# Row variance of the later layer norms from a centred square on ScalarE, in place of a raw square and two small VectorE operations

## The chip, the cores and the metric

The kernel runs on one core of a Trainium2 chip. A core has five engines that run their own instruction queues: TensorE (PE, matrix products; its weight loads are listed apart as PEld), VectorE (DVE), ScalarE (ACT), GpSimd (POOL) and SyncE (SP, which issues most of the DMAs). They wait for one another through semaphores. The metric is the device time of one execution in microseconds. The kernel before took 319.8 us, the median of three runs (319.6 to 320.18).

## The reference

The input x has 2048 rows of 512 numbers (bf16). Four layers follow each other, each of the form x = x + layer(norm(x)), in the order A, B, A, B with the same weights for both A and both B layers. The norm is what the change touches:

```python
def _layernorm(x, axis=-1, eps=1e-5):
    m = jnp.mean(x, axis=axis, keepdims=True)
    v = jnp.var(x, axis=axis, keepdims=True)
    return (x - m) / jnp.sqrt(v + eps)
```

Layer A is linear attention with 32 heads of 16 channels: q, k and v from one projection, q and k multiplied by a small matrix per head and passed through two softmaxes (of the values and of their negatives), then products of the features with v, a division by the denominators, and an output product. Layer B is sliding-window attention: each position looks at itself and seven earlier positions, two apart, with a softmax over the eight, and an output product. The result is x after the fourth layer.

## The kernel before

The rows are cut into four blocks of 512 rows, and a block into four tiles of 128 rows (one row per partition). All of x stays on chip. Every layer is a set of stages per block: a norm, projections, the attention's own steps, and an output product that adds the residual. The stages of a layer are a1 (k, v and the sums over rows), a2 (q), a3 and a4 (denominators and output) for A, and b1 (q, k, v), b2 (scores and softmax), b3 (values) for B. The output product of all layers is `s_out` (line 531). For every layer but the last it also gathers what the next layer's norm needs, so there are twelve such norms: three layer boundaries of four blocks. The first layer's norms get their statistics in another way (`s_ln_first`) and are not touched.

In `s_out`, for each of a block's four tiles t: `mm` multiplies on TensorE into a bank of PSUM; `res` adds the residual and writes x back, on VectorE (line 571) or, where TensorE has added the residual by an identity product (line 556), on ScalarE (line 568). Both also leave the row's sum in one column of `sums`. `sq` (line 574) squares the tile on ScalarE and leaves the row's sum of squares in a column of `ss`; it waits for `res`. The squared tile itself, `sqd`, is thrown away. After the four tiles, `var` (line 584) forms ss - sums * sums / 512 for all four columns on VectorE with two operations on 128x4 numbers. `s_norm` (line 443) goes on: `ln` takes the logarithm of the variance plus eps and an exponential with factor -0.5 on ScalarE (lines 450 and 453), which gives rstd; `nmr` forms -mean * rstd on VectorE (line 457); `ap` writes the normalised tile xn, on VectorE (line 466) or ScalarE (line 468); then xn is transposed to xnT, by a DMA from the SP queue (line 473) or by TensorE (line 482) with copies out of PSUM (lines 202 and 204). The projections of the next layer read xnT.

ScalarE and VectorE share the copies out of PSUM (`copy`, lines 202 and 204); a string of digits, `_CHOICE`, fixes for each copy which of the two does it. PSUM has eight banks, and another string, `_SLOTS`, gives each product its bank; a product waits until the bank's earlier content has been read. ScalarE also does all exponentials (lines 638, 745, 1073) and VectorE the large products of layer B (lines 1059 and 1121).

The order of each engine's work is written out by hand: `_ORDER` (line 60) is a list of 1492 tokens, each the next step of one named thread, and an engine takes its instructions in the order of that list. A stage's steps on one engine form a thread; `var` and `nmr` of a norm are two tokens of the same thread.

Of the kernel before, what the change touches and what calls it, by code (L numbers as in the profile page):

```python
# [60 lines left out]
8 2 i 2e 3s e3 ce 2p 23 i a 5l i i 9 i i i 5o i i i i 4e e7 1m i 0 3u 3r 0 f i e c j b 2 k 3 4 j o 5q 1m l 3 m
p 1n 0 i 1 n 1t e4 o 1o q 1m 1p r 0 1m 1u s 1m z 5k z z 5 1m 1r 7 6 z 20 20 7 1q 1s 1t 21 21 t 20 20 1v 22 10
z 22 1t 7 1t 20 1w 22 t 11 24 24 13 u 12 16 12 1t t 15 1t v 12 12 22 x 18 14 1x d w w 1y 2c y 18 18 26 18 2d
1f 2d 2c 1z 2d 24 2d 27 17 19 18 1a 1b 21 1c 1d 22 21 22 39 1e 20 20 22 39 25 2c 3b 3a 3a 1f 3a 2d 3a 2f 2c 1f
1f 39 ch 22 2f 2d 2g 1g 29 1f 2d 1j 2f 2d 7 1h 29 1i 1k 3a 29 2n 29 2i 2n 3c 2o 2o 2o 2k 2o 2k 2q 1l cd 2h 2n
2a 2k 2f 2n 2k 3a 2o 2j 24 2q 2r 2q 2o 2o 2o 29 2y 28 2y 2y 3c 2l 2z 2v 2z 2s 2z 2z 2k 2y 2z 39 36 31 2z 36 2z
3a 3b 36 36 2v 31 2v 37 2v 31 2t 36 2z 36 2b 2b 2b 2b 2m 2m ci 36 36 2m 3a 2w 2m 2v 33 34 32 31 3c 35 2q 3c 36
3b 2x g 2x 2u 2x 30 37 2x 36 38 38 38 38 3i 3c 3h 3c 39 3b 3a 3j 3k 3k 3k 3c 3d 3c 3e 3l 3b 3m 3d 3e 5h 3n 3m
3c 3e 3e 3l 5i 3m 3q 3m 3m 4f 3m 3d 3l 5j 3e 3e 3m 5i 3m 3m 3v 3d 3e 3e bd 5h 5m 5n 5i 5i 5i 3m 3d 3e 7c 5h 7d
5p 5i 5i 5i 5r 3f 3g 3g 5i 3f 3g 5i 3w 3f 3z 3x 3f 3g 5s 3y 7e 40 41 3g 7d 5u 5v 7f 5t 3g 3p 41 42 41 41 44 3g  # L70
43 3g 43 5w 5x 5x 7f 45 46 43 43 47 43 7f 5y 3f 90 47 48 49 3g 4c 91 5x 41 4b 41 41 41 4a 92 5x 4d 60 91 4l 5z
61 5z 93 5z 4q 62 5z 4g 7d 4g 4g 4m 4q 63 ck 5z 7d 4r 93 4i 4l 63 66 64 67 7g 4s 7j 65 7h 7i 4h 4j 7k bo 4n 4q
4q 4u 4w 91 7l 4t 7l 7l 7m 7l 7o 68 7n 7n 4l 7p 3h 7n 7q 4w 93 4v 7n 4v 3o 91 4f 6a 7r 4o 6b 7n 6k 6f 69 4g 4k
4l 7r 6l 7s h 4w 6g 6k 6m 4p 6a 6c 6p 7t 7u 6a 6k 6f 6n 7v 4w 6k 6h 94 6r 6d 4x 4x b2 6r 4x 97 6o 98 4x 95 6f
69 7x 96 99 99 9a 4y 6i 99 7w 9b 6q 9c 6q 9d 9b 9b 99 9e 9b 6r 6a 6e 6f 6j 83 84 d4 6q 7y 9f 7y 9b 6r 6s 6s 6s
6s 9f 9h 9i 4y 9g 4w 8d 80 9j 7z 6t 6t 3t 88 6s 83 89 6t 88 88 88 8a 8b 8f 8c 7y 6r 7x 4x 9l 6u 9k 6u 4y 6u 4w
6q 6u 83 85 83 86 87 81 9r 9w 7y 9w 9s 9x 4v 82 4v 9w 6v 9y 9z 4z a1 6v 4z 6v 6w 4z 8e 6v 4z 6y 9m 6x 6z 70 9n
70 70 71 72 73 70 9m 74 72 72 8e 9m 50 50 50 75 50 9o 72 51 9r 52 76 53 8f 54 55 72 9p 9w 76 8f 79 55 77 7a 9r
9t 55 58 78 7b 9u 55 9r 56 9m 8f 59 8g 57 5a 57 8e 8g a3 8g 8g 57 bz b0 8e 9q 57 9v a0 5b 57 8h a3 5b bz 8h a3
8g 5d c0 5e 5c 5f c0 c0 b0 c0 bz 8h b1 5g b3 b1 8f b0 b1 b3 a2 b1 a4 c0 b1 a4 b1 a3 a4 a2 a4 b4 b5 a5 bz a5 8i  # L80
8i c0 8i a2 b3 a4 a2 c0 bx b6 c0 b3 a5 by bx by by b0 b7 bx by by by a3 8i bx 8j 8j b1 8j 8l a6 8k 8j 8m b1 8n
ap by aq aq ap a6 aq aq 8o 8o 8p by 8r 8o 8o 8q 8s 8q as 8t 8q as ap 8q au as ap a6 8u 8q a7 aq at 8u 8w aq bz
a7 8v a7 aq aq 8x 8y 8z bx a9 a6 a7 a8 b8 aa as ax b8 ab ac ac c0 aw by ad ac ac b8 ax b8 ae be af av ah bb bb
bb b9 ag ae bb b8 bf ae ae c1 ai bc bc ae bc ar be ax bc bc bc bc bc ax ay ai aj ac ak am ac an ac al ac be bm
ao bn bm bj bn bm bn bp ax bn bu bu bu c2 bu bj bj bn bg c2 c1 bm bn be az az bv bn az az ba bj ba ba bn bu bk
bu ba bj bu bu c1 c2 c2 c2 c1 bp c2 bl bl bh bl bu bq bp bp br bi bv bl bw bw bs bu iw bt bw bw c2 c7 c8 ix c9
c2 c9 c1 c2 c9 ca c3 cb iw cc cb fp c4 ca fq c3 cb c4 ca cf cb cb cg cb c4 fr c4 cb cj e0 fq c3 fs fs cb cb c3
fs c5 c4 c4 c4 cb c4 cl e1 e2 cm c3 e1 e0 cp cn co e1 e6 e1 cq e5 e0 c4 e1 e1 c5 cq e8 e1 e1 e9 ea cq e1 cr e1
eb cu h9 ee ct ec ef fq cq fq ed eg cs cs cv cs cs ha eh eg ft hb fu fv eg ha hc hc fw hc eg fx fy fy cw el fy
ei cs cw cy cx cq cq d0 ej ek cq d1 cq ei fy d2 fz cz d3 ei ei g3 df df em g1 df g0 ei em eo dh c6 da ep en eq  # L90
dg g2 di df dj g0 d5 ha d5 g0 d4 d6 da g0 g4 er dk d5 dk ha db g0 dc g4 es g6 hd d8 hh he da i7 dk d5 hf hg hi
dl g5 g7 d7 d9 i7 g8 hi hj dd hi hl hk hk hm hi hn hk hk ho hk ho hp et hr f3 eu et da ey dl ev ey ey hs de hq
dl f4 f1 et dl ez ey ht ew f2 f0 f3 f5 f3 dm g9 f8 dm dm f6 dm dn dk i1 fa i1 fa i2 dn i3 dl i6 i6 gq f3 f7 es
i6 i9 et f9 i6 i9 i6 i6 f9 dm hu ex fa ga i9 ia dn id i6 hv i1 fb fb fa fb fb fc i4 i1 i5 i6 dl c6 i6 do fc i9
ie ib i6 do hw hx do fb gg i6 f9 fc gl i6 i6 i6 gm i6 ic hu i8 dp i6 ic dp dr dp dq gh ds ic hw f9 gg gg ic gi
hy ic ic gl ic gl ic fa gn gb ic ic do fd fd c5 ic go ic ic hw hw ic hz gb fd ic dp gc fe i0 gj gs fe gd fe if
dt ff if if fh ig gb if ig gg ig gl gs ge gs fg ig gk gb gp gt gr gr gr gt ga gf ih ih if ig if ig du gr if if
gs ih du ig dv gt ii gt dw fd ig ij ij ii ik gu gu ij du gt du ij dy ik ih gu fe gs dz il gv fi gv ii ij ij im
ik il fj fk fj dx in fl iq fj ir fj dx fo iq fm is ii gw gw ij gv il ij gx ik gw il io gv gv fn fm iy gz iq ip
iq iu it gy iv it h2 gw h0 gw h2 iz h3 h4 h5 h3 h1 h2 h6 h3 h2 h3 h5 h7 h5 h8 iy h5 j0  # L100
"""


# [33 lines left out]
class _Fast:  # L137
# [393 lines left out]
    def s_out(self, st, key, b, Wo, last, lhs=None):  # L531
        nc, add = self.nc, self.step
        xb = self.x[b]
        T = {}
# [39 lines left out]
        def sq(t):  # L574
            if "ss" not in T:
                T["ss"] = self.sm([4], "ss")
            sqd = self.t2([D], "sqd")
            nc.scalar.activation(out=sqd[:], in_=xb[:, t, :], func=ACT.Square, accum_out=T["ss"][:, t:t + 1])  # L578
# [4 lines left out]

        def var(lo, n):
            if "q" not in T:
                T["q"] = self.sm([4], "q")
# [1 line left out]
            nc.vector.scalar_tensor_tensor(out=T["q"][:, lo:lo + n], in0=u, scalar=-1.0 / D, in1=u,
                                           op0=ALU.mult, op1=ALU.mult)
            nc.vector.tensor_tensor(out=T["q"][:, lo:lo + n], in0=T["q"][:, lo:lo + n],  # L590
                                    in1=T["ss"][:, lo:lo + n], op=ALU.add)
# [1534 lines left out]
```

## Time and profile before

| what | value |
| --- | --- |
| device time, median of 3 runs | 319.8 us (319.6 to 320.18) |
| profiled execution, first to last instruction | 318.1 us |
| its own time by that median | 1.7 us above the span |
| PE / DVE / ACT busy | 307.7 / 295.6 / 275.0 us |
| PE clock granted | full in all of the span |

The profile is of one execution. Its span counts from the first instruction to the last, and the device time has some more around it; 319.8 - 318.1 = 1.7 us is taken for that, as the profiled execution's device time is not given apart. Busy time is the union of an engine's instructions. In lists of groups, a line reads: source line, engine, operation, what is written from what, shapes, count, then busy time in us, mean of one in ns, and the idle time just before. In a timeline, a line begins with the start in us and the duration in us of an instruction or a run of like ones; an idle time before it stands in brackets with what ended it. In lists of waits, a line gives who waited for whom, the sum in us, the number of times and the longest. In lists by stage, a line gives the stretch in us, its length, each engine's busy time with its count of instructions, the granted clock, the DMA engines' share and GB/s.

### The profile page before, as it was taken

How to read it: one execution, taken by the hardware profiler on the slowest of the kernel's cores; microseconds unless marked ns; L12 is line 12 of the kernel's file. 1: busy time of each engine (PE TensorE's matmuls, PEld its weight loads, DVE VectorE, ACT ScalarE, POOL GpSimd, SP SyncE). 2: the span in 40 equal slices, each digit the busy share in tenths (PEclk: the TensorE clock that was granted, in tenths of full speed). 3: DMA queues.
4: the chain of work that ended last, by engine and by line, in shares of the span. 5: the costliest groups of instructions: out<-in, count | busy, mean ns of one | idle time of the engine just before them, and what ended most of it. 6: DMA issues, size and time to landing. Idle time of an engine off the chain costs nothing.

```text
span 318.1 us, 8900 instructions
## 1 busy us (share of the span) xinstructions
PE 307.7 (97%) x3578; PEld 152.9 (48%) x3578; DVE 295.6 (93%) x459; ACT 275.0 (86%) x639; POOL 47.2 (15%) x60
## 2 busy tenths in 40 slices
PE   8999999899999999999999999989999999999994
PEld 4644456445454444444444455544444544444552
DVE  6999996998999999999999999689998999999994
ACT  4999999999898778999999999899999867697751
POOL 6000000000004212000000000033141644045000
PEclk9999999999999999999999999999999999999999
DMA  7977100005794989939894600004289875565664
GB/s 203 358 186 148 36 2 4 2 19 145 165 178 100 156 141 136 144 66 140 145 134 62 69 0 2 4 19 134 59 185 137 140 133 134 105 178 126 158 152 170
DMA packets 45789, 36.37 MB, mean 114 GB/s; under 512 B 30832, under 2 KB 41136, under 8 KB 45744
## 3 DMA queue, kind: packets, MB, share of 16 engines
q1 hardware_dynamic: 45216, 35.75, 56.3%
q8 instruction: 29, 0.48, 0.7%
q14 instruction: 16, 0.13, 0.2%
q10 hardware_dynamic: 528, 0.02, 0.1%
HBM read 11.13 MB, written 3.25 MB: 45 GB/s over the span
## 4 chain that ended last, share of the span: by engine, by line
PE 87%; DVE 5%; ACT 5%; DMA 1%; issue 1%; SPq 0%; DVEq 0%; ACTq 0%
PE PS L967 23%; PE PS L553 18%; PE PS L632 9%; PE PS L644 9%; PE PS L737 6%; PE PS L1128 4%; PE PS L1066 4%; PE PS L1185 2%; DVE Eq L855 2%; PE PS L707 2%; PE PS L940 1%; PE PS L482 1%; PE PS L556 1%; PE PS L1200 1%; PE PS L1082 1%; DMA x<-in_A_x_dram 1%
## 5 line engine op out<-in xcount | busy, mean ns | idle before, releaser
L967 PE MATMUL PS<-xnT,WB 128*128 128x512 bf16 x336 | 76.8, 380 | 0.1
L1059 DVE TENSOR_TENSOR prod<-QT,K 128x4096 bf16<-128x4096 bf16 x28 | 63.4, 2287 | 0.5 <-POOL K L993 0.5
L1121 DVE TENSOR_TENSOR pav<-PT,Vg 128x4096 bf16<-128x4096 bf16 (+1 forms) x29 | 62.9, 2214 | 0.2
L967 PEld LDWEIGHTS <-WB 128*128 128x128 bf16 x336 | 37.3, 114 | 36.4 <-issue 3.3
L745 ACT ACTIVATE Eq<-PS 128x512 bf16<-128x512 f32 x64 | 36.3, 619 | 0.0
L638 ACT ACTIVATE Ek<-PS 128x512 bf16<-128x512 f32 x64 | 35.1, 622 | 0.2 <-PE PS L632 0.2
L553 PEld LDWEIGHTS <-oT 128*128 128x128 bf16 x236 | 21.9, 98 | 26.6 <-issue 1.3
L737 PE MATMUL PS<-xnT,WA 128*128 128x512 bf16 x128 | 32.0, 380 | 0.5 <-DVE s L829 0.3
L578 ACT ACTIVATE sqd<-x 128x512 bf16<-128x512 bf16 x48 | 29.9, 631 | 2.2 <-DVE x L571 2.0
L644 PE MATMUL PS<-WA,xnT 128*128 128x512 bf16 x128 | 31.6, 379 | 0.0
L632 PE MATMUL PS<-WA,xnT 128*128 128x512 bf16 x128 | 31.0, 379 | 0.2 <-ACT WA L204 0.2
L571 DVE SCALAR_TENSOR_TENSOR x<-PS,x 128x512 bf16<-128x512 f32 x46 | 30.2, 684 | 0.7 <-PE PS L553 0.7
L204 ACT CAST oT<-PS 128x512 bf16<-128x512 f32 (+1 forms) x50 | 26.7, 597 | 3.8 <-PE PS L1128 2.1
L553 PE MATMUL PS<-WoA,oT 128*128 128x512 bf16 x128 | 29.8, 380 | 0.0
L553 PE MATMUL PS<-WoB,oT 128*128 128x512 bf16 x108 | 26.5, 379 | 0.0
L204 ACT CAST K<-PS 128x512 bf16<-128x512 f32 x30 | 17.3, 593 | 3.1 <-PE PS L967 1.9
L632 PEld LDWEIGHTS <-xnT 128*128 128x128 bf16 x128 | 12.3, 98 | 15.2 <-issue 1.0
L644 PEld LDWEIGHTS <-xnT 128*128 128x128 bf16 x128 | 12.2, 98 | 14.5 <-issue 0.4
L690 DVE TENSOR_TENSOR Ek<-Ek,rk 128x4096 bf16<-128x4096 bf16 (+1 forms) x10 | 18.6, 1860 | 0.4 <-ACT rk L685 0.4
L737 PEld LDWEIGHTS <-WA 128*128 128x128 bf16 x128 | 11.6, 98 | 14.6 <-issue 1.7
L466 DVE TENSOR_SCALAR xn<-x,rstd,nmr 128x512 bf16<-128x512 bf16 x48 | 18.1, 424 | 0.6
L204 ACT CAST V<-PS 128x512 bf16<-128x512 f32 x26 | 15.2, 596 | 2.6 <-PE PS L967 2.6
(175 smaller groups left out, 505.1 us busy)
## 6 DMA issues: line engine op xcount, KB each, us to landing
Vg<-V SPq DMA_DIRECT2D x112, 131.5 KB, 4.3
Prho<-rd SPq DMA_DIRECT2D x8, 512.0 KB, 6.1
x<-in_A_x_dram SPq DMA_DIRECT2D x3, 512.0 KB, 6.6
WB<-in_B_wqkv_dram SPq DMA_DIRECT2D x3, 512.0 KB, 9.8
out_dram<-x SPq DMA_DIRECT2D x6, 256.0 KB, 2.3
wraw<-in_A_wqkv_dram SPq DMA_DIRECT2D x4, 256.0 KB, 4.5
vd<-Vs SPq DMA_DIRECT2D x2, 272.0 KB, 2.9
x<-in_A_x_dram SPq DMA_DIRECT2D x4, 128.0 KB, 3.4
```

The source lines that it names most:

```text
L204: self.nc.scalar.copy(out=out, in_=in_)
L553: nc.tensor.matmul(y[:], lhsT=lh(t, c), rhs=Wo()[:, c, :], start=(c == 0), stop=(c == NB - 1 and not onpe))
L571: nc.vector.scalar_tensor_tensor(out=xb[:, t, :], in0=T[t][:], scalar=1.0, in1=xb[:, t, :], op0=ALU.mult, op1=ALU.add, **kw)
L578: nc.scalar.activation(out=sqd[:], in_=xb[:, t, :], func=ACT.Square, accum_out=T["ss"][:, t:t + 1])
L632: nc.tensor.matmul(pk[:], lhsT=xnT[:, t, k, :], rhs=self.WA[:, k, D:2 * D], start=(k == 0), stop=(k == NB - 1))
L638: nc.scalar.activation(out=T["E"][:, t, s, :], in_=T["k", t][:], func=ACT.Exp, scale=1.0 - 2.0 * s)
L644: nc.tensor.matmul(pv[:], lhsT=xnT[:, t, k, :], rhs=self.WA[:, k, 2 * D:3 * D], start=(k == 0), stop=(k == NB - 1))
L737: nc.tensor.matmul(pq[:], lhsT=self.WA[:, k, hb * P:(hb + 1) * P], rhs=xnT[:, :, k, :], start=(k == 0), stop=(k == NB - 1))
L745: nc.scalar.activation(out=self.Eq[L, b][s][:, :, hb, :], in_=T[hb][:].rearrange("p (t i) -> p t i", t=4), func=ACT.Exp, scale=1.0 - 2.0 * s)
L967: nc.tensor.matmul(pp[:], lhsT=self.WB[:, k, i * D + c:(i + 1) * D:NB], rhs=xnT[:, :, k, :], start=(k == 0), stop=(k == NB - 1))
L1059: nc.vector.tensor_tensor(out=pr[:], in0=QT[:, c:c + 1, :].to_broadcast([P, NW, TB]), in1=win, op=ALU.mult)
L1121: nc.vector.tensor_tensor(out=pv, in0=PT[:, :, lo:lo + n].unsqueeze(1).to_broadcast([P, NB, 2, n]), in1=vw, op=ALU.mult)
```

## The change

The square takes a scale and a bias: it forms (sums - 512 * x) squared, which is 512 squared times the square of x minus its row's mean. Its row sum in `ss` is then 512 cubed times the variance, so `var` and its tile `q` go, and `ln` reads `ss` with the factor 1/512 cubed in place of 1/512. The bias is a column of `sums`, one number per partition. Twelve tokens, one per norm, leave `_ORDER`; all others stay in their order.

```diff
@@ s_out
         def sq(t):
...
             sqd = self.t2([D], "sqd")
-            nc.scalar.activation(out=sqd[:], in_=xb[:, t, :], func=ACT.Square, accum_out=T["ss"][:, t:t + 1])
+            nc.scalar.activation(out=sqd[:], in_=xb[:, t, :], func=ACT.Square, scale=-float(D),
+                                 bias=T["sums"][:, t:t + 1], accum_out=T["ss"][:, t:t + 1])
...
-        def var(lo, n):
-            if "q" not in T:
-                T["q"] = self.sm([4], "q")
-            u = T["sums"][:, lo:lo + n]
-            nc.vector.scalar_tensor_tensor(out=T["q"][:, lo:lo + n], in0=u, scalar=-1.0 / D, in1=u,
-                                           op0=ALU.mult, op1=ALU.mult)
-            nc.vector.tensor_tensor(out=T["q"][:, lo:lo + n], in0=T["q"][:, lo:lo + n],
-                                    in1=T["ss"][:, lo:lo + n], op=ALU.add)
-
         def norm(lo, n):
-            add(st, "DVE", var, lo, n)
-            V = {"var": lambda: T["q"][:, lo:lo + n], "sum": lambda: T["sums"][:, lo:lo + n]}
-            self.s_norm(st, key, b, V, tuple(range(lo, lo + n)), 1.0 / D, 1.0 / D)
+            V = {"var": lambda: T["ss"][:, lo:lo + n], "sum": lambda: T["sums"][:, lo:lo + n]}
+            self.s_norm(st, key, b, V, tuple(range(lo, lo + n)), 1.0 / D, 1.0 / D ** 3)
```

More of the change, by code (lines that the diff above doesn't have):

```diff
@@ L60 @@
 _ORDER = """
[L61 to L100, printed above, removed]
+8 2 i 2e 3s e3 ce 2p 23 i a 5l i i 9 i i i 5o i i i i 4e e7 1m i 0 3u 3r 0 f i e c j b 2 k 3 4 j o 5q 1m l 3 m p
@@ new lines @@
+1n 0 i 1 n 1t e4 o 1o q 1m 1p r 0 1m 1u s 1m z 5k z z 5 1m 1r 7 6 z 20 20 7 1q 1s 1t 21 21 t 20 20 1v 22 10 z 22
+1t 7 1t 20 1w 22 t 11 24 24 13 u 12 16 12 1t t 15 1t v 12 12 22 x 18 14 1x d w w 1y 2c y 18 18 26 18 2d 1f 2d 2c
+1z 2d 24 2d 27 17 19 18 1a 1b 21 1c 1d 22 21 22 39 1e 20 20 22 39 25 2c 3b 3a 3a 1f 3a 2d 3a 2f 2c 1f 1f 39 ch
+22 2f 2d 2g 1g 29 1f 2d 1j 2f 2d 7 1h 29 1i 1k 3a 29 2n 29 2i 2n 3c 2o 2o 2o 2k 2o 2k 2q 1l cd 2h 2n 2a 2k 2f 2n
+2k 3a 2o 2j 24 2q 2r 2q 2o 2o 2o 29 2y 28 2y 2y 3c 2l 2z 2v 2z 2s 2z 2z 2k 2y 2z 39 36 31 2z 36 2z 3a 3b 36 36
@@ new lines @@
+2v 31 2v 37 2v 31 2t 36 2z 36 2b 2b 2b 2b 2m 2m ci 36 36 2m 3a 2w 2m 2v 33 34 32 31 3c 35 2q 3c 36 3b 2x g 2x 2u
+2x 30 37 2x 36 38 38 38 38 3i 3c 3h 3c 39 3b 3a 3j 3k 3k 3k 3c 3d 3c 3e 3l 3b 3m 3d 3e 5h 3n 3m 3c 3e 3e 3l 5i
+3m 3q 3m 3m 4f 3m 3d 3l 5j 3e 3e 3m 5i 3m 3m 3v 3d 3e 3e bd 5h 5m 5n 5i 5i 5i 3m 3d 3e 7c 5h 7d 5p 5i 5i 5i 5r
+3f 3g 3g 5i 3f 3g 5i 3w 3f 3z 3x 3f 3g 5s 3y 7e 40 41 3g 7d 5u 5v 7f 5t 3g 3p 41 42 41 41 44 3g 43 3g 43 5w 5x
+5x 7f 45 46 43 43 43 7f 5y 3f 90 47 48 49 3g 4c 91 5x 41 4b 41 41 41 4a 92 5x 4d 60 91 4l 5z 61 5z 93 5z 4q 62
@@ new lines @@
+5z 4g 7d 4g 4g 4m 4q ck 5z 7d 4r 93 4i 4l 63 66 64 67 7g 4s 7j 65 7h 7i 4h 4j 7k bo 4n 4q 4q 4u 4w 91 7l 4t 7l
+7l 7m 7l 7o 68 7n 7n 4l 7p 3h 7n 7q 4w 93 4v 7n 4v 3o 91 4f 6a 4o 6b 7n 6k 6f 69 4g 4k 4l 7r 6l 7s h 4w 6g 6k 6m
+4p 6a 6c 6p 7t 7u 6a 6k 6f 6n 7v 4w 6k 6h 94 6r 6d 4x 4x b2 6r 4x 97 6o 98 4x 95 6f 69 7x 96 99 99 9a 4y 6i 99
+7w 9b 6q 9c 6q 9d 9b 9b 99 9e 9b 6r 6a 6e 6f 6j 83 84 d4 6q 7y 7y 9b 6r 6s 6s 6s 6s 9f 9h 9i 4y 9g 4w 8d 80 9j
+7z 6t 6t 3t 88 6s 83 89 6t 88 88 88 8a 8b 8f 8c 7y 6r 7x 4x 9l 6u 9k 6u 4y 6u 4w 6q 6u 83 85 83 86 87 81 9r 9w
@@ new lines @@
+7y 9w 9s 9x 4v 82 4v 9w 6v 9y 9z 4z a1 6v 4z 6v 6w 4z 8e 6v 4z 6y 9m 6x 6z 70 9n 70 70 71 72 73 70 9m 74 72 72
+8e 9m 50 50 50 75 50 9o 72 51 9r 52 53 8f 54 55 72 9p 9w 76 8f 79 55 77 7a 9r 9t 55 58 78 7b 9u 55 9r 56 9m 8f
+59 8g 57 5a 57 8e 8g a3 8g 8g 57 bz b0 8e 9q 57 9v a0 57 8h a3 5b bz 8h a3 8g 5d c0 5e 5c 5f c0 c0 b0 c0 bz 8h
+b1 5g b3 b1 8f b0 b1 b3 a2 b1 a4 c0 b1 a4 b1 a3 a4 a2 a4 b4 b5 a5 bz a5 8i 8i c0 8i a2 b3 a4 a2 c0 bx b6 c0 b3
+a5 by bx by by b0 b7 bx by by by a3 8i bx 8j 8j b1 8j 8l a6 8k 8j 8m b1 8n ap by aq aq ap a6 aq aq 8o 8o 8p by
@@ new lines @@
+8r 8o 8o 8q 8s 8q as 8t 8q as ap 8q au as ap a6 8q a7 aq at 8u 8w aq bz a7 8v a7 aq aq 8x 8y 8z bx a9 a6 a7 a8
+b8 aa as ax b8 ab ac ac c0 aw by ad ac ac b8 ax b8 ae be af av ah bb bb bb b9 ag ae bb b8 bf ae ae c1 bc bc ae
+bc ar be ax bc bc bc bc bc ax ay ai aj ac ak am ac an ac al ac be bm ao bn bm bj bn bm bn bp ax bn bu bu bu c2
+bu bj bj bn bg c2 c1 bm bn be az az bv bn az az ba bj ba ba bn bu bk bu ba bj bu bu c1 c2 c2 c2 c1 bp c2 bl bl
+bh bl bu bq bp bp br bi bv bl bw bw bs bu iw bt bw bw c2 c7 c8 ix c9 c2 c9 c1 c2 c9 ca c3 cb iw cc cb fp c4 ca
@@ new lines @@
+fq c3 cb c4 ca cf cb cb cg cb c4 fr c4 cb cj e0 fq c3 fs fs cb cb c3 fs c5 c4 c4 c4 cb c4 cl e1 e2 cm c3 e1 e0
+cp cn co e1 e6 e1 cq e5 e0 c4 e1 e1 c5 cq e8 e1 e1 e9 ea cq e1 cr e1 eb cu h9 ee ct ec ef fq cq fq ed eg cs cs
+cv cs cs ha eh eg ft hb fu fv eg ha hc hc fw hc eg fx fy fy el fy ei cs cw cy cx cq cq d0 ej ek cq d1 cq ei fy
+d2 fz cz d3 ei ei g3 df df g1 df g0 ei em eo dh c6 da ep en eq dg g2 di df dj g0 d5 ha d5 g0 d4 d6 da g0 er dk
+d5 dk ha db g0 dc g4 es g6 hd d8 hh he da i7 dk d5 hf hg hi dl g5 g7 d7 d9 i7 g8 hi hj dd hi hl hk hk hm hi hn
@@ new lines @@
+hk hk hk ho hp et hr f3 eu et da ey dl ev ey ey hs de hq dl f4 f1 et dl ez ey ht ew f2 f0 f3 f5 f3 dm g9 f8 dm
+dm f6 dm dn dk i1 fa i1 fa i2 dn i3 dl i6 i6 gq f3 f7 es i6 i9 et f9 i6 i9 i6 i6 f9 dm hu ex fa ga i9 ia dn id
+i6 hv i1 fb fb fa fb fb fc i4 i1 i5 i6 dl c6 i6 do fc i9 ie ib i6 do hw hx do fb gg i6 f9 fc gl i6 i6 i6 gm i6
+ic hu i8 dp i6 ic dp dr dp dq gh ds ic hw f9 gg gg ic gi hy ic ic gl ic gl ic fa gn gb ic ic do fd fd c5 ic go
+ic ic hw hw ic hz gb fd ic dp gc fe i0 gj gs fe gd fe if dt ff if if fh ig gb if ig gg ig gl gs ge gs fg ig gk
@@ L101 @@
+gb gp gt gr gr gr gt ga gf ih ih if ig if ig du gr if if gs ih du ig dv gt ii gt dw fd ig ij ij ii ik gu gu ij
+du gt du ij dy ik ih gu fe gs dz il gv fi gv ii ij ij im ik il fj fk fj dx in fl iq fj ir fj dx fo iq fm is ii
+gw gw ij gv il ij gx ik gw il io gv gv fn fm iy gz iq ip iq iu it gy iv it h2 gw h0 gw h2 iz h3 h4 h5 h3 h1 h2
+h6 h3 h2 h3 h5 h7 h5 h8 iy h5 j0
 """
```

## The prediction

> **What bounds the kernel now.** The page comes first: its span, the busy line, the granted clock and the head of the chain that ended last.
>
> ```profile
> span 318.1 us, 8900 instructions
> ...
> PE 307.7 (97%) x3578; PEld 152.9 (48%) x3578; DVE 295.6 (93%) x459; ACT 275.0 (86%) x639; POOL 47.2 (15%) x60
> ...
> ACT  4999999999898778999999999899999867697751
> ...
> PEclk9999999999999999999999999999999999999999
> ...
> PE 87%; DVE 5%; ACT 5%; DMA 1%; issue 1%; SPq 0%; DVEq 0%; ACTq 0%
> ```
>
> TensorE (PE) is busy for 97% of the span, at the full clock, and holds 87% of the chain. So the kernel is as long as TensorE's work plus the holes in it. An edit to VectorE (DVE) or ScalarE (ACT) changes the time only by what it adds to, or takes from, those holes. The average hides where the other engines have air, so the second view is the busy time by stage, first of everything and then of the square's line alone (a count of 8 there is four squares and four reads of the accumulator).
>
> ```profile
> 68.00:95.00 27.00, 26.99 (x225) 13.70 (x224) 25.45 (x58) 24.32 (x59) 0.86 (x3) 1.00 0.68 149
> 95.00:128.00 33.00, 33.00 (x251) 15.67 (x250) 32.83 (x33) 27.07 (x61) 8.07 (x9) 1.00 0.84 133
> 128.00:140.00 12.00, 12.00 (x80) 5.61 (x79) 11.90 (x10) 11.37 (x30) 0.00 (x0) 1.00 0.62 87
> 140.00:196.00 56.00, 56.00 (x477) 25.75 (x477) 55.00 (x74) 55.17 (x134) 0.39 (x1) 1.00 0.62 87
> 215.00:247.00 32.00, 31.89 (x302) 15.44 (x302) 29.38 (x71) 30.62 (x81) 8.24 (x7) 1.00 0.67 130
> ```
>
> ```profile
> 128.00:140.00 12.00, 2.78 (x8) 1.00 0.62 87
> 140.00:196.00 56.00, 8.18 (x24) 1.00 0.62 87
> 215.00:247.00 32.00, 10.83 (x32) 1.00 0.67 130
> ```
>
> The columns are the stretch, its length, then busy time of PE, PEld, DVE, ACT and POOL. PE has no hole between 68 and 196 us. ACT has 2.68 us of air in the first row and 5.93 in the second, but only 0.63 + 0.83 = 1.46 us in 128 to 196 and 1.38 us in 215 to 247. 4 + 12 + 16 = 32 of the 48 squares lie in those two tight stretches.
>
> **The change part by part.** First the rows that price it: instructions by line, with busy time and the mean of one in ns.
>
> ```profile
> L578 ACT ACTIVATE sqd<-x 128x512 bf16<-128x512 bf16 x48 | 29.9, 631 | 2.2 <-DVE x L571 2.0
> L468 ACT ACTIVATE xn<-x,nmr,rstd 128x512 bf16<-128x512 bf16 x16 | 12.9, 818 | 0.2 <-DVE nmr L457 0.2
> L835 ACT ACTIVATE Ds<-Ds,deneps_t 128x128 f32<-128x128 f32 x8 | 3.3, 413 | 1.1 <-DVE Ds L832 1.0
> L836 ACT ACTIVATE Ds<-Ds 128x128 f32<-128x128 f32 x8 | 2.5, 309 | 0.2
> L590 DVE TENSOR_TENSOR q<-q,ss 128x4 f32<-128x4 f32 x12 | 2.0, 168 | 2.5 <-ACT sqd L578 1.5
> L588 DVE SCALAR_TENSOR_TENSOR q<-sums 128x4 f32<-128x4 f32 x12 | 1.9, 162 | 0.1
> ```
>
> *Added: a per-partition bias on 48 squares.* The square has neither bias nor scale tensor now; after the change it reads one column of `sums` (the scale is an immediate). No such square is in the trace. The nearest row is L468: same line length, same types, with two such operands, 818 ns against the square's 631, so (818 - 631) / 2 = 94 ns for each. L835 against L836, same shape with one operand more (another function too), gives 413 - 309 = 104. I take 97. Below, the cost is bounded by nothing (if the read hides under the instruction in front), above by 104. Whether it hides is read from how closely instructions follow each other:
>
> ```profile
> 137.01 2.23 ACT L468 ACTIVATE xn<-x,nmr,rstd 128x512 bf16<-128x512 bf16 x3
> ...
> 141.56 0.62 ACT L578 ACTIVATE sqd<-x 128x512 bf16<-128x512 bf16 x1
> 142.08 0.19 ACT L578 ACTIVATION_READ_ACCUMULATOR sqd<-x 128x1 f32 x1
> 142.18 0.62 ACT L578 ACTIVATE sqd<-x 128x512 bf16<-128x512 bf16 x1
> ```
>
> Three L468 take 2.23 us, so they start (2.23 - 0.82) / 2 = 0.71 us apart; a square is followed after 142.08 - 141.56 = 0.52 us. The difference of 0.19 us for two operands is the whole of their price: it is not hidden. So 48 x 97 ns = 4.7 us go onto ACT's queue. The Trainium skill, "ScalarE: Activation LUTs", section "What ACT_TABLE_LOAD costs", gives 93 ns for each pointer operand and says that back-to-back ACTIVATEs overlap by about 93 ns. Taken together, one could read that as an operand that costs the queue nothing, and the time would stay at 319.8; the 0.71 against 0.52 us above speaks against that reading.
>
> The square already waits for the residual that makes x; the same instruction, or its accumulator read, makes the sum. So no other engine is newly waited for.
>
> *Removed: 24 small DVE operations and one hop between engines.*
>
> ```profile
> 79.72 0.16 DVE L588 SCALAR_TENSOR_TENSOR q<-sums 128x4 f32<-128x4 f32 x1
> 79.98 0.16 DVE L590 TENSOR_TENSOR q<-q,ss 128x4 f32<-128x4 f32 x1
> 80.09 1.23 DVE L875 TENSOR_TENSOR Eq<-Eq,Prho 128x2048 bf16<-128x2048 bf16 x1
> ...
> 245.75 0.22 ACT L578 ACTIVATION_READ_ACCUMULATOR sqd<-x 128x1 f32 x1
> 246.01 0.16 DVE L590 TENSOR_TENSOR q<-q,ss 128x4 f32<-128x4 f32 x1 [0.79 <-ACT sqd L578]
> 246.21 0.30 ACT L450 ACTIVATE lnv<-q,eps_t 128x4 f32<-128x4 f32 x1 [0.23 <-DVE q L590]
> ```
>
> A pair holds DVE from 79.72 to 80.09, 0.37 us with the wait between them; twelve free 4.4 us of DVE. That work is hidden by PE today: in 68 to 196 us PE has no hole for an earlier DVE to close. Taken at nothing. The stall of 0.79 us at 246.01 does not go either: DVE meets the next wait, of `nmr` for ScalarE's rstd, a little later in its own queue.
>
> The hop is worth something on ACT: ln at 246.21 starts 0.24 us after the last accumulator read ends (245.75 + 0.22); read directly from ACT, I estimate 0.03 (ln to exp on ACT follow that closely: 246.21 + 0.30, then 246.53). ACT's idle time for q, in all:
>
> ```profile
> ACT lnv L450 <- DVE q L590: 1.2, 4, 0.5
> ```
>
> So at most 1.2 us of ACT idle goes, against 4.7 us added. Per norm, four squares in a row end 0.39 us later and the hop gives back at most some 0.2: the chain to the normalised rows is about 0.2 us longer where the hop was waited for, 0.4 where it was not. The transposing DMAs on the SP queue, and the transfers behind them, issue later by as much; nothing on PE's chain waits for them in the stretches above (DMA is 1% of the chain).
>
> *What of ACT's lateness reaches PE.* Here the sum is made. PE waits for ACT's copies out of PSUM where the bank is needed again, and for ACT's share of the transposes. The copies at 140.19 and 176.03 free such a bank, the one at 228.98 makes a part of a projection's transposed input:
>
> ```profile
> 140.19 0.57 ACT L204 CAST K<-PS 128x512 bf16<-128x512 f32 x1
> 140.81 1.02 PE L553 MATMUL PS<-WoB,oT 128*128 128x512 bf16 x4
> 140.98 0.60 ACT L568 ACTIVATE x<-PS 128x512 bf16<-128x512 f32 x1 [0.22 <-PE PS L556]
> ...
> 176.03 1.08 ACT L204 CAST oT<-PS 128x512 bf16<-128x512 f32 x2
> 176.68 0.38 PE L644 MATMUL PS<-WA,xnT 128*128 128x512 bf16 x1
> ...
> 189.86 2.07 ACT L638 ACTIVATE Ek<-PS 128x512 bf16<-128x512 f32 x4 [0.18 <-PE PS L632]
> ...
> 228.98 1.01 ACT L204 COPY xnT<-PS 128x1024 bf16<-128x1024 bf16 x1
> 230.18 0.79 PEld L967 LDWEIGHTS <-WB 128*128 128x128 bf16 x5 [0.41 <-DVE xnT L202]
> ```
>
> The copy at 140.19 ends at 140.76 and the matmul starts at 140.81. Of the pair at 176.03, the first ends near 176.60 (a lone copy takes 0.57 in the first row) and the matmul starts at 176.68. Neither has slack: 0.05 and 0.08 us lie between copy and matmul. At 230.18 the slack behind ACT's half is 0.19 us. So lateness of ACT passes to PE at these places nearly one for one, though the page shows no PE wait there.
>
> The terms: (1) 68 to 128 us: four squares before 73 us give 0.39 - 0.2 = 0.2 late, and the slack takes half: 0.1; the rest vanishes in ACT's 8.6 us of air. (2) 128 to 196: the first four squares bring 0.39 us against 0.63 + 0.22 us of air up to 141 us; ACT waits for PE there and is on time again soon after, but the copy at 140.19 stands between, so I count 0.2. The other twelve bring 1.16 us. Of the air of 0.83 us in that stage, 0.22 is the wait at 140.98, before them, 0.18 the wait at 189.86, and the rest, 0.43, lies in short pieces, partly between dependent instructions; I count 0.18 and half of the 0.43 as absorbing, 0.4 together. 0.2 + 1.16 - 0.4 = 1.0 (rounded). (3) 215 to 247: twelve of the 16 squares start before 237 us, 1.16 us; of the air of 1.38 us I take 0.8 as real, as in (2), and the slack of 0.19 at 230.18 goes off too: 0.2. (4) 247 on: ACT has air (its row of tenths falls to 6 and 7 there), 0. (5) Removed work on the chain: 0.
>
> Sum: 0.1 + 1.0 + 0.2 = 1.3 us. The profiled execution spans 318.1 us; 318.1 + 1.3 = 319.4. The runs' median is 319.8 us, 1.7 above that span for what lies around it: 319.4 + 1.7 = 321.1.
>
> **The rivals.**
>
> *Hidden after all, 319.8.* PSUM has eight banks and the order leaves slack at most places; if ACT's air in 128 to 196 us is real air (1.46 against 1.55), only 0.1 us passes there, the second stretch passes nothing, and the time stays within 0.3 us of now. For it: PE's rows are full to the hundredth there, so no wait on ACT has grown to a hole yet. Against: 140.81 and 176.68.
>
> *ACT becomes the bound, 322.5.* In the two tight stretches every square's 97 ns reaches PE: (16 + 12) x 0.097 = 2.7 us, 319.8 + 2.7. For it: ACT is at 55.17 of 56.00 us. Against: 1.46 and 1.38 us of air, and DVE's rows are as full, so the order alternates between who is late.
>
> *Faster, 317.9.* DVE, not PE, paces 95 to 196 us (32.83, 11.90 and 55.00 of 33, 12 and 56 us). Five norms have their pair there; 5 x 0.37 = 1.85 us earlier at DVE would move the time to 319.8 - 1.85. It decides only if PE has holes before matmuls that wait for DVE's products there; PE is at 33.00, 12.00 and 56.00, so what can be gained is only in starts too short to show as idle.
>
> **How the numbers follow.** A measurement of this kernel tells a change of about 0.2%, 0.64 us, from none. Chances: the forecast (320.5 to 321.9) 0.60; ACT as bound (321.9 to 323) 0.14; hidden 0.20; faster 0.06. Slower by over 0.2% is 0.60 + 0.14 = 0.74, same 0.20, faster 0.06. The range goes from 319.6, which takes in the hidden case, to 322.6, just over the whole cost of the tight stretches; what lies below and above holds some 0.15. The likeliest case's own range is 320.5 to 321.9.
>
> **What would show it.** Right: the square's mean at 631 + 97, about 728 ns, still x48; L588 and L590 gone; ln reading ss; DVE's busy time down by about 24 x 0.165 = 4.0 us and its share falling; ACT's up by 4 to 5 us; ACT above 55.5 of 56 us in the stage that starts near 140; new PE idle rows released by ACT copies, or starts of matmuls that move by some 0.3 us at the output product near 141 and by some 1.0 us near 177. Wrong: a square that stays at 631 ns (then 319.8 or less), PE without new holes, or a first stage (68 to 128 us) that already loses more than 0.5 us, which would mean that the chain of a single norm, not ACT's load, is what counts.

## The result and the profile after

The changed kernel takes 320.63 us, the median of 20 runs (320.06 to 321.3), against 319.87 us for the kernel before in the same session (20 runs, 319.41 to 320.78). The ratio is 1.0021 with an interval of 1.0014 to 1.0028, which is 0.67 us (0.45 to 0.90) at 319.87 us. So the change is slower, as forecast, but by half of the 1.3 us that the sum gave: 321.1 us was forecast, within 319.6 to 322.6.

Below the first lines of the page of the changed kernel: the span, the busy times, and the head of the chain that ended last.

```profile
span 319.0 us, 8873 instructions
...
PE 308.2 (97%) x3578; PEld 153.2 (48%) x3578; DVE 293.0 (92%) x435; ACT 278.7 (87%) x639; POOL 47.8 (15%) x60
...
PE 66%; ACT 19%; DVE 9%; POOL 1%; issue 1%; DMA 1%; SPq 0%; ACTq 0%; DVEq 0%
```

The span is 0.9 us longer (319.0 against 318.1). DVE is 2.6 us less busy, with 459 - 435 = 24 instructions fewer; ACT is 3.7 us more busy with the same 639. What PE has lost in the chain, 87% to 66%, went to ACT (5% to 19%) and DVE (5% to 9%). PE itself still shows next to no idle time, so the chain says more than the busy line: a part of it now runs through ACT's queue where it ran through PE's before.

The groups of instructions that the change touches (source line, operation, tiles and shapes, count, busy time in us, mean of one in ns, idle time before):

```profile
L578 ACT ACTIVATE sqd<-x,sums 128x512 bf16<-128x512 bf16 x48 | 34.6, 736 | 1.7 <-DVE x L571 1.6
L578 ACT ACTIVATION_READ_ACCUMULATOR sqd<-x,sums 128x1 f32 x48 | 10.1, 211 | 0.0
L450 ACT ACTIVATE lnv<-ss,eps_t 128x4 f32<-128x4 f32 x12 | 3.8, 315 | 0.1
```

The square went from 631 to 736 ns, 105 ns more. L588 and L590 are gone. `ln` reads `ss` and has 0.1 us of idle time in front, where ACT had waited 1.2 us for `q`. So each part of the change does what it says.

By stage, with the columns of the prediction (stretch, length, busy PE, PEld, DVE, ACT, POOL, clock, DMA share, GB/s):

```profile
68.00:95.00 27.00, 26.99 (x225) 13.61 (x223) 24.70 (x52) 25.56 (x60) 0.87 (x3) 1.00 0.62 149
95.00:128.00 33.00, 33.00 (x252) 15.79 (x250) 32.72 (x31) 27.09 (x60) 7.99 (x9) 1.00 0.84 133
128.00:140.00 12.00, 12.00 (x80) 5.61 (x79) 11.80 (x8) 11.46 (x30) 0.00 (x0) 1.00 0.62 87
140.00:196.00 56.00, 55.83 (x420) 25.21 (x418) 53.96 (x66) 55.63 (x133) 0.39 (x1) 1.00 0.62 87
215.00:247.00 32.00, 31.05 (x302) 14.98 (x299) 28.52 (x62) 31.57 (x80) 9.85 (x8) 1.00 0.67 123
```

PE's first idle time shows in the row of 140 to 196 us (55.83 of 56.00): three holes of 0.07, 0.07 and 0.04 us, ahead of the matmuls at 141.21, 176.73 and 177.39 us that are shown below. (The last row's PE fell from 31.89 to 31.05 for another reason: a wait of 0.95 us that ended at 215.11 before and ends at 215.99 now has moved into the stretch.) From 140 to 196 us ACT rose from 55.17 to 55.63 and DVE fell from 55.00 to 53.96. ACT is full; DVE, which was relieved, stands. The list of DVE's waits says where, first before and then after (who waited for whom, sum in us, times, longest):

```profile
DVE q L590 <- ACT sqd L578: 1.5, 2, 0.8
...
DVE nmr L457 <- ACT rstd L453: 0.6, 1, 0.6
```

```profile
DVE nmr L457 <- ACT rstd L453: 5.6, 6, 1.9
```

The stall at `q` (1.5 us) is gone, and the next wait in DVE's queue, `nmr` for rstd, grew from 0.6 to 5.6 us. So 5.0 - 1.5 = 3.5 of the 4.4 us that the pair held are now spent waiting.

Where the time came from shows in the starts of the same instruction in both traces. Each row gives how much later than in the kernel before PE starts the matmul that began there at the named time; the offset that the execution already had at 70 us (between 0.09 and 0.48 us, nearly all of it from its first 15 us) is taken off. Each row is of one execution; where two kernels are still the same, as the last row and the kernel before up to 141.5 us, they differ by 0.01 us. The trace of centred_b0_b1 (see the experiments) lacks 29 records of matmuls, and its row goes by the weight loads:

```
start before, us     80     130    141.5   165    172    176.3   190    246
the change         +0.16  +0.08  +0.27  +0.18  +0.28  +0.54  +0.73  +0.63
operand_alone      +0.34  +0.29  +0.47  +0.37  +0.48  +0.71  +0.89  +0.91
removal_alone       0.00  -0.09  -0.12  -0.28  -0.21  -0.21  -0.26  -0.38
centred_a1          0.00  +0.01  +0.20  +0.13  +0.23  +0.48  +0.68  +0.70
centred_b0_b1      +0.15  +0.06  +0.06  +0.05  +0.05  +0.05  +0.05  +0.20
load_elsewhere      0.00   0.00  +0.01  +1.07  +1.23  +1.23  +1.26  +1.26
```

The change loses 0.08 us up to 130 us, 0.65 from there to 190, and gains 0.10 back by 246: 0.63 us up to there, close to the measured 0.67. Behind it the traces part once more, at a wait of PE near 292 us: 0.50 us before, 0.74 with the change, 0.35 with the operand alone and 0.77 with the removal alone. What makes it is open, and it is in none of the sums below. Two places in the timeline of the changed kernel (start and duration in us) carry most of the middle term:

```profile
140.58 0.58 ACT L204 CAST K<-PS 128x512 bf16<-128x512 f32 x1
141.21 1.02 PE L553 MATMUL PS<-WoB,oT 128*128 128x512 bf16 x4
141.77 0.71 ACT L578 ACTIVATE sqd<-x,sums 128x512 bf16<-128x512 bf16 x1
142.38 0.19 ACT L578 ACTIVATION_READ_ACCUMULATOR sqd<-x,sums 128x1 f32 x1
142.47 0.71 ACT L578 ACTIVATE sqd<-x,sums 128x512 bf16<-128x512 bf16 x1
...
171.83 0.69 DVE L202 CAST vaug<-PS 128x512 bf16<-128x512 f32 x1
173.54 0.16 DVE L457 SCALAR_TENSOR_TENSOR nmr<-sums,rstd 128x4 f32<-128x4 f32 x1 [1.02 <-ACT rstd L453]
174.39 2.28 DVE L1112 TENSOR_TENSOR pav<-PT,Vg 128x4096 bf16<-128x4096 bf16 x1
176.73 0.61 PE L1119 MATMUL PS<-pav,indAV 128*32 128x512 bf16 x8
177.39 1.02 PE L635 MATMUL PS<-WA,xnT 128*128 128x512 bf16 x4
```

The copy that began at 140.19 begins at 140.58, and the matmul behind it at 141.21 in place of 140.81: 0.40 later, 0.13 of it the execution's offset. The square is followed by its read after 142.38 - 141.77 = 0.61 us, 0.52 before. Near 172 us DVE stands 1.02 us at `nmr`, and behind it in its queue is the product `pav`, which the matmul at 176.73 reads. The matmul that began at 176.68 before begins at 177.39, 0.71 later (0.58 without the offset). The prediction named this place, but only with ACT's copy of oT ahead of it. Of the 0.65 us, 0.19 came at 141 us and 0.29 at 176 to 177; the other large step is 0.15 at 187 us, ahead of PE's transposes of xn.

### The profile page after: what moved, and what is told of

Same layout as the page of the kernel before. It is cut to its first block, busy times and chain, and to the rows that moved or that the text cites. A ratio compares the mean times of both kernels' runs of the same rounds, so it can differ in the third digit from the quotient of the medians.

```text
span 319.0 us, 8873 instructions
## 1 busy us (share of the span) xinstructions
PE 308.2 (97%) x3578; PEld 153.2 (48%) x3578; DVE 293.0 (92%) x435; ACT 278.7 (87%) x639; POOL 47.8 (15%) x60
## 4 chain that ended last, share of the span: by engine, by line
PE 66%; ACT 19%; DVE 9%; POOL 1%; issue 1%; DMA 1%; SPq 0%; ACTq 0%; DVEq 0%
PE PS L958 20%; PE PS L553 14%; PE PS L635 6%; PE PS L623 5%; ACT Eq L736 3%; PE PS L728 3%; PE PS L1119 3%; ACT sqd L578 3%; PE PS L1057 2%; PE PS L1176 2%; DVE Eq L846 2%; ACT Ek L629 2%; DVE Ek L681 2%; POOL vh L1000 1%; PE PS L931 1%
## 5 line engine op out<-in xcount | busy, mean ns | idle before, releaser
L578 ACT ACTIVATE sqd<-x,sums 128x512 bf16<-128x512 bf16 x48 | 34.6, 736 | 1.7 <-DVE x L571 1.6
L728 PEld LDWEIGHTS <-WA 128*128 128x128 bf16 x128 | 11.7, 98 | 14.6 <-issue 1.7
```

The lines of the kernel that those rows point to most:

```text
L728: nc.tensor.matmul(pq[:], lhsT=self.WA[:, k, hb * P:(hb + 1) * P], rhs=xnT[:, :, k, :], start=(k == 0), stop=(k == NB - 1))
```

## The experiments

**The operand alone.** The kernel before, its pair on VectorE kept, with a bias of zeros on all 48 squares.

```diff
-            nc.scalar.activation(out=sqd[:], in_=xb[:, t, :], func=ACT.Square, accum_out=T["ss"][:, t:t + 1])
+            nc.scalar.activation(out=sqd[:], in_=xb[:, t, :], func=ACT.Square, bias=self.zero_t[:, 0:1],
+                                 accum_out=T["ss"][:, t:t + 1])
```

> The kernel before, with one edit: each of the 48 squares reads a per-partition bias from a column of zeros, so the raw square and the two VectorE operations stay. Theory (ScalarE's added time is the whole loss, and the freed VectorE gives a little back): the square's mean goes from 631 to about 733 ns, ScalarE gets 4.7 us more, and the time rises by 0.9 us (0.7 to 1.2), more than the whole change's 0.7. Rival (the loss comes from the removed pair, because VectorE now stands earlier and longer at the wait for rstd): the time stays within 0.2 us of before.

Measured: 320.54 us against 319.82, ratio 1.0026 (1.0014 to 1.0039), that is +0.83 us; by the starts +0.91. Its group of squares:

```profile
L580 ACT ACTIVATE sqd<-x,zero_t 128x512 bf16<-128x512 bf16 x48 | 34.6, 736 | 2.1 <-DVE x L573 2.0
```

The same 736 ns as in the changed kernel: the price hangs on the operand's being there, not on what it holds. The operand alone explains all of the loss; that it costs a little more than the whole change shows only in the starts (0.91 against 0.63), since the two intervals overlap.

**The removal alone.** The changed kernel with the raw square back.

```diff
-            nc.scalar.activation(out=sqd[:], in_=xb[:, t, :], func=ACT.Square, scale=-float(D),
-                                 bias=T["sums"][:, t:t + 1], accum_out=T["ss"][:, t:t + 1])
+            nc.scalar.activation(out=sqd[:], in_=xb[:, t, :], func=ACT.Square, accum_out=T["ss"][:, t:t + 1])
```

> The kernel after, with the square back to its raw form without bias or scale; the pair of VectorE operations stays out. The logarithm reads the sum of squares over 512, so the square of the mean is left out of the variance. Theory: VectorE loses 24 operations, ScalarE gets nothing more, and the time falls by 0.25 us (0 to 0.5). Rival (the loss comes from the removed pair): the time rises by some 0.7 us, as with the whole change.

Measured: ratio 0.9993 (0.9982 to 1.0004). The interval holds 1, so the time by itself decides nothing on the sign of the gain; it excludes that taking the pair away costs 0.7 us. PE's starts say more: -0.38 us, in steps before matmuls that read DVE's products (111.6 and 163.5 us) and, by 246, behind the second tight stretch. Together, +0.91 - 0.38 = +0.53 us, against +0.63 for the change. DVE's wait for rstd is there without any operand:

```profile
DVE nmr L457 <- ACT rstd L453: 3.5, 5, 1.6
```

**Only the norms ahead of the second layer A.** Four norms, 16 squares, in 128 to 196 us; the other eight as before.

```diff
+CENTRED = ('A1',)
...
+            if key in CENTRED:
+                nc.scalar.activation(out=sqd[:], in_=xb[:, t, :], func=ACT.Square, scale=-float(D),
+                                     bias=T["sums"][:, t:t + 1], accum_out=T["ss"][:, t:t + 1])
```

> The kernel before, with the change made only in the four norms in front of the second layer A (16 squares, 128 to 185 us, where ScalarE has the least air); the other eight norms keep the raw square and the pair. Theory (the loss arises in the tight stretch): the time rises by 0.5 us (0.3 to 0.7), three quarters of the whole change's loss from a third of its squares. Rival (each norm's longer chain costs alike): a third, 0.2 us.

Measured: 320.73 us, ratio 1.0030 (1.0019 to 1.0040); by the starts +0.70. A third of the squares bring all of the loss.

**Only the norms ahead of the two layers B.** The other eight norms, 32 squares (`CENTRED = ('B0', 'B1')` in the same edit).

> The kernel before, with the change made only in the eight norms in front of the two layers B (32 squares, 69 to 109 us and 220 to 246 us); the four norms in front of the second layer A keep the raw square and the pair. Theory (what is lost is lost in the tight stretch from 128 to 196 us, the rest is air and a little VectorE relief): within 0.3 us of before. Rival (each square costs alike): two thirds of the whole change's loss, 0.5 us.

Measured: 320.22 us against 320.26, ratio 1.0004 (0.9992 to 1.0016). Two thirds of the squares cost nothing that the time can tell. By the starts it is +0.20: 0.15 at 75 us, as in the whole change, and a wait of PE of 0.25 us near 235 us which the whole change does not have, less what the removal gives back. The two runs together settle where most of the loss arises: in the stage where ACT had 1.46 us of air for 16 squares' 1.5 us.

**The same load at another place.** The kernel before with a bias of zeros on 16 exponentials of the second layer A (147 to 168 us), its squares raw.

```diff
-                                 func=ACT.Exp, scale=1.0 - 2.0 * s)
+                                 func=ACT.Exp, scale=1.0 - 2.0 * s,
+                                 **({"bias": self.zero_t[:, 0:1]} if L == 1 and b < 2 else {}))
```

> The kernel before, norms untouched; 16 exponentials of the second layer A's first two blocks (147 to 168 us) get a bias column of zeros. ScalarE gets 16 x 97 ns = 1.55 us in the tight stretch, outside the norms' chains. Theory (what counts is the load on ScalarE's queue, wherever in the stretch it is put): the time rises by 0.8 us (0.5 to 1.2), as much as or more than with the 16 squares of that stretch. Rival (what counts is the longer chain from residual to normalised rows): within 0.2 us of before.

Measured: 321.4 us, ratio 1.0048 (1.0034 to 1.0062), that is +1.5 us; by the starts +1.26. More than expected. The groups of exponentials without and with the operand:

```profile
L747 ACT ACTIVATE Eq<-PS 128x512 bf16<-128x512 f32 x48 | 27.1, 611 | 0.0
...
L747 ACT ACTIVATE Eq<-PS,zero_t 128x512 bf16<-128x512 f32 x16 | 10.6, 730 | 0.0
```

At 93 ns in the queue, 16 operands are 1.5 us, and nearly all of it arrives. So load on ACT's queue in this stretch is enough for a loss, without a longer norm and without any part of the variance. It does not show that the squares' loss came by load alone: of their 0.65 us, the steps at 176 us (behind `nmr`) and 187 us (xn) lie behind a norm. That this load passes nearly whole, and the squares' only by 0.65 of 1.5 us, is a matter of place: 1.07 us had reached PE by 165 us. Which slack the squares use and the exponentials don't was not tried.

**A second operand.** The changed kernel with its scale as a column, too.

```diff
-            nc.scalar.activation(out=sqd[:], in_=xb[:, t, :], func=ACT.Square, scale=-float(D),
+            nc.scalar.activation(out=sqd[:], in_=xb[:, t, :], func=ACT.Square, scale=self.negd_t[:, 0:1],
```

> The kernel after, with the scale -512 read from a per-partition column as well, so that each of the 48 squares has two such operands. Theory (97 ns of ScalarE queue for each operand; once ScalarE's air in 128 to 196 us is used up, every further piece passes to TensorE): the square's mean goes to some 830 ns, and the time rises to 2.5 us above before (1.8 to 3.5), so the second operand costs more than the first. Rival (the first operand's loss is a single new wait): the second one costs 0.3 us at most, and the time stays 1 us above before.

```profile
L580 ACT ACTIVATE sqd<-x,sums,negd_t 128x512 bf16<-128x512 bf16 x48 | 39.1, 828 | 1.8 <-DVE x L573 1.7
```

Measured: 322.32 us against 320.26, ratio 1.0074 (1.0056 to 1.0093), +2.4 us. The second operand has the price of the first in its row (828 - 736 = 92 ns), but 2.4 - 0.7 = 1.7 us in the time, where the first brought 0.7. The first used up the air; the second found little left: from 130 to 190 us its traced execution loses 0.44 to 2.35, 1.9 us, against 0.65 with one operand, so the second brings some 1.26 of its 16 x 93 ns = 1.5 us. That comes close to the prediction's rival "ACT becomes the bound", one operand later than it was feared.

**Work moved to DVE, after and before.** Since DVE was relieved, four pieces that ACT does were given to it in the changed kernel: the xn tiles near 75 and 139 us and the vaug copies near 172 and 183 us. The same move was made in the kernel before, as a control.

```diff
-...10100001100111010001000000000011011111100"
+...10100001101111010001000000000011011111100"
```

(The first of the four digits of `_CHOICE`; the other three change in the same way.)

> The kernel after, with four pieces of ScalarE's work given to VectorE at places where VectorE now stands idle or has time freed: one normalised tile in front of 75 us, one near 139 us, and two copies of values near 172 and 183 us, in front of the waits for rstd. ScalarE gets 2.4 us less, VectorE 1.9 us more. Theory: ScalarE's lateness in the tight stretch was the loss, so most of it goes: the time comes to before or 0.3 us below (-0.6 to +0.3). Rival (VectorE has no room and becomes late itself): at or above the time of after, 0.7 us above before or more.

> The kernel before, with the same four pieces given to VectorE, where VectorE still has the pair of operations per norm. Theory (the freed VectorE time is what takes these pieces): VectorE is full at 55.00 of 56 us, so nothing is gained: within 0.4 us of before. Rival (ScalarE's lateness costs the kernel before as well): 0.5 us or more below before.

Measured: 323.32 us after (ratio to before 1.0100, 1.0082 to 1.0118) and 324.07 before (1.0117, 1.0097 to 1.0137). Both theories failed, and in the changed kernel the rival came out: the move costs 3.2 - 0.7 = 2.5 us there and 3.7 us in the kernel before. By the starts, 0.85 us of it come at 75 us in both kernels, and 1.7 and 2.4 us near 175 us. PE's waits with the move in the changed kernel, and DVE's queue near 175 us:

```profile
PE PS L1119 <- ACT Ek L629: 1.0, 1, 1.0
PE PS L482 <- DVE xn L466: 0.8, 1, 0.8
...
PE PS L1119 <- DVE pav L1112: 0.6, 1, 0.6
```

```profile
172.66 0.69 DVE L202 CAST vaug<-PS 128x512 bf16<-128x512 f32 x1 [1.97 <-PE PS L635]
173.27 2.28 DVE L1112 TENSOR_TENSOR pav<-PT,Vg 128x4096 bf16<-128x4096 bf16 x1
...
176.07 0.15 DVE L457 SCALAR_TENSOR_TENSOR nmr<-sums,rstd 128x4 f32<-128x4 f32 x1
```

At 75 us PE waits for the very tile that was moved: xn reads `nmr`, so it lies behind DVE's idle time there and cannot use it. Near 175 us the moved copy stands ahead of a large product `pav` in DVE's queue and waits 1.97 us for the matmul that makes its input; that `pav` starts at 173.27 us in place of 169.62 (1.0 us of it was there before), and `nmr`, the next `pav` and PE come late behind it. So the move failed by the places in the queue that the pieces got. That DVE has no room for such a piece anywhere is not shown.

**The logarithm ahead of a copy.** If DVE's stand at `nmr` near 172 us is the way to PE, rstd should come sooner: ACT's vaug copy is put behind the logarithm there.

```diff
-... as ap 8q au as ap a6 8q a7 aq at 8u ...
+... as ap 8q as ap a6 8q au a7 aq at 8u ...
```

The two orders are of the changed kernel: `8q` issues the last square and the logarithm, `au` the copy, `8u` is `nmr`. A control makes the move in the kernel before.

> The changed kernel; one copy of vaug on ScalarE near 172.3 us is moved behind the logarithm and the exponential of the third block's norm. In the changed kernel VectorE stands 1.02 us at nmr there, with the product pav behind it, and the matmuls from 176.08 us on come 0.24 us later. Theory (that stand is the way to those matmuls): rstd is ready 0.47 us earlier, the stand falls to about 0.55 us, pav starts 0.47 us earlier, and the whole is 0.1 to 0.25 us shorter than the changed kernel: 0.4 to 0.55 us above the kernel before (ratio 1.0013 to 1.0017). Rival (ScalarE's own load is the way, in its copies behind): no change against the changed kernel, ratio 1.002. A third: the copy that is moved back by 0.8 us holds its bank, and the time goes up by up to 0.5 us more, ratio up to 1.0037.

> The same move in the kernel before. There VectorE does not stand at nmr at this place. Theory: nothing is gained, 0 to +0.3 us by the later copy, ratio 1.0000 to 1.0010. Rival (the moved copy is what counts): the same step as in the changed kernel.

Measured: 320.81 us, ratio 1.0039 (1.0026 to 1.0053), and 320.61 us for the control, 1.0020 (1.0008 to 1.0031), against 319.99 us. Nothing was gained; by the starts the changed kernel is 0.15 us later at 246 us with the move than without it. That is nearest to the third expectation, but not by the bank that it named. In the control the move costs 0.6 us for a reason that the changed kernel doesn't have: without the copy ahead of it, ACT stands 0.56 us at the logarithm for `q`. The timeline of the first shows the place:

```profile
173.11 0.16 DVE L457 SCALAR_TENSOR_TENSOR nmr<-sums,rstd 128x4 f32<-128x4 f32 x1 [0.68 <-ACT rstd L453]
...
173.96 2.29 DVE L1112 TENSOR_TENSOR pav<-PT,Vg 128x4096 bf16<-128x4096 bf16 x1
...
176.41 0.60 PE L1119 MATMUL PS<-pav,indAV 128*32 128x512 bf16 x8
177.44 1.02 PE L635 MATMUL PS<-WA,xnT 128*128 128x512 bf16 x3 [0.43 <-ACT oT L204]
```

DVE's stand fell from 1.02 to 0.68 us, `pav` came 0.43 us earlier, and the matmul that reads it 0.32 earlier (176.41 for 176.73); 0.10 of each is the offset between these two executions. So that way exists. But the next matmul still starts at 177.44 (177.39 without the move): it now waits 0.43 us for ACT's copy of oT. Both ways to this place were late by the same ACT queue, and closing one shows the other. In the control the matmul at 176.68 starts at 177.37, also behind that copy.

**The variance on GpSimd.** The kernel before, raw square, with three small GpSimd operations in place of DVE's two.

```diff
-            nc.vector.scalar_tensor_tensor(out=T["q"][:, lo:lo + n], in0=u, scalar=-1.0 / D, in1=u,
-                                           op0=ALU.mult, op1=ALU.mult)
-            nc.vector.tensor_tensor(out=T["q"][:, lo:lo + n], in0=T["q"][:, lo:lo + n],
-                                    in1=T["ss"][:, lo:lo + n], op=ALU.add)
+            nc.gpsimd.tensor_tensor(out=q, in0=u, in1=u, op=ALU.mult)
+            nc.gpsimd.tensor_scalar(out=q, in0=q, scalar1=-1.0 / D, scalar2=None, op0=ALU.mult)
+            nc.gpsimd.tensor_tensor(out=q, in0=q, in1=T["ss"][:, lo:lo + n], op=ALU.add)
```

> The kernel before, with the variance formed on GpSimd by three small operations (a product, a scaling, a sum) in place of VectorE's two; the square stays raw, without an operand. Theory (the loss is the operand on ScalarE, and VectorE's freed 4.4 us is worth 0.2 to 0.35 us): the operand is not paid, VectorE is freed, but three operations at some 0.2 us and more on GpSimd, and a hop, make rstd about 0.5 us later at twelve norms, so between -0.3 and +0.5 us, ratio 0.9990 to 1.0016. Rival (what counts is how long a norm takes from its last square to rstd): slower than the changed kernel, over +0.7 us, ratio over 1.0021.

```profile
L589 POOL TENSOR_TENSOR q<-sums 128x4 f32<-128x4 f32 x12 | 13.3, 1109 | 93.2 <-DVE x L571 52.8 <-ACT x L568 40.4
...
L590 POOL TENSOR_SCALAR q<-q 128x4 f32<-128x4 f32 x12 | 10.4, 863 | 1.1
L450 ACT ACTIVATE lnv<-q,eps_t 128x4 f32<-128x4 f32 x12 | 3.6, 296 | 9.5 <-POOL q L591 9.5
L591 POOL TENSOR_TENSOR q<-q,ss 128x4 f32<-128x4 f32 x12 | 2.6, 213 | 3.4 <-ACT sqd L578 2.7
```

Measured: 331.74 us, ratio 1.0361 (1.0345 to 1.0377). Far above the theory's range and on the rival's side. The three operations take 1109 + 863 + 213 ns on average, against 162 + 168 on DVE, and ACT stands 9.5 us at the logarithm for them (1.2 us before). This doesn't decide between load and length of a norm at the small size that was in question. With norms that are some 2 us longer the length is the likely cause of the loss, but no run separates it from what GpSimd and VectorE do to each other (last section). Of the 331.7 - 320.0 = 11.7 us the span holds 326.5 - 318.1 = 8.4; the rest lies outside it.

No version here is faster than the kernel before by more than the measurement tells; the norms ahead of layers B alone can be changed at no cost that the time can tell.

## Why the prediction was right in direction and wrong in size

*What bounds the kernel: right.* PE is at the full clock throughout, and the loss is lateness that ACT hands to PE. It passes one for one where the prediction said so: without the offset, the copy of oT that began at 176.03 starts 0.57 us later, and the matmul behind it, which began at 176.68, 0.58.

*Price of the operand: right.* 97 ns was taken; the starts give 0.61 - 0.52 = 0.09 us, the means 736 - 631 = 105 ns. The Trainium skill, "ScalarE: Activation LUTs", section "What ACT_TABLE_LOAD costs", has 93 ns for a pointer operand, and the trace agrees (93 ns between starts: the median distance from a square to the next instruction is 520, 613 and 706 ns with none, one and two operands; 92 for the second operand's mean). The reading by which the overlap of instructions would hide it was rightly refused.

*The hop: right.* ACT's 1.2 us at `ln` went to 0.1.

*Term (1), 68 to 128 us, forecast +0.1: right, in part by luck.* +0.16 at 80 us, +0.08 at 130. The fall between the two is the 0.09 us that the removal gave back at 111.6 us, which the prediction took at nothing; the operand alone stands at +0.29 there.

*Term (2), 128 to 196 us, forecast +1.0: the mis-sized term, +0.65.* Its first part was right: 0.2 was counted for the copy at 140.19, and 0.27 - 0.08 = 0.19 arrived. The forecast of ACT's own lateness was nearly right too. It was to be on time again behind its wait at 140.98, and then 1.16 - 0.4 = 0.76 us late. Without the offset, its square at 141.56 starts 0.07 us later than before, and its instructions behind the wait at 189.86 us 0.73 later: the twelve squares added 0.66 of their 12 x 93 ns = 1.1 us, and 0.46 was absorbed, of it 0.22 at the wait at 189.86 that the prediction named. The step that failed is the sum 0.2 + 0.76. PE stays late by the 0.2 us of the copy at 140.19 while ACT is on time again, so the first 0.2 us that ACT falls behind after it cost PE nothing: PE is late by as much already. At 190 us both are 0.73 us late, of it 0.08 from before 130 us. So these two delays of one engine, with a wait of it between them, did not add; the larger one counted.

*Term (3), 215 to 247 us, forecast +0.2: wrong in sign, -0.10.* The square's load there brought +0.02 with the pair kept (0.91 - 0.89), and the removal -0.12 (0.38 - 0.26). In these two kernels ACT's 1.38 us of air took the twelve squares whole; with only the norms ahead of layers B changed, they brought 0.15 there.

*Term (5), removed work on DVE, "taken at nothing": wrong.* The step was that PE has no hole that an earlier DVE could close. Rows of PE that are full to the hundredth hid waits of about 0.1 to 0.2 us: without the pair PE starts 0.38 us earlier by 246 us, 0.09 of it at 111.6, 0.16 at 163.5 and 0.12 at 238.5 us. This is the mechanism of the rival "faster", at a fifth of the 1.85 us that it was given.

*The stall that moves: right, and more than was made of it.* That DVE would meet the wait of `nmr` next was said, but only as a reason for no gain. It is also why so little of the relief reaches PE in the tight stage: in the changed kernel DVE's copy that began at 172.16 us starts 0.33 us earlier than in the kernel before, and `nmr`, the next in its queue, which began at 172.84, 0.70 later. What DVE had gained it lost there, on rstd from ACT.

The sum by the measured terms is 0.08 + 0.65 - 0.10 = 0.63 us, against 0.1 + 1.0 + 0.2 = 1.3.

*The signs.* The square's mean (736 ns for 728), ACT in the stage from 140 us (55.63 for over 55.5) and the start near 141 us (+0.27 for 0.3) came as named. Near 177 us the start moved by 0.58 and not 1.0. DVE's busy time fell by 2.6 and not 4.0 us, though the rows of the pair held 2.0 + 1.9 = 3.9: busy time is a union, and neighbouring records overlap. ACT's rose by 3.7 and not 4 to 5.
